# Loading two of batch 0's head pairs in two stretches and computing the first-half exponentials first, in a fused attention and feed-forward kernel

## The chip, the cores and the metric

The kernel runs on one core of one Trainium2 chip. The metric is the device time of one execution in microseconds (us). Shorter is better. All runs told here were fast runs: the kernel uses one core, and no run lay over 1.5% above the fastest of its kernel.

The engines are named as in the profile: PE is TensorE's matmul, PEld its weight load, DVE VectorE, ACT ScalarE, POOL GpSimd. "The granted clock" is TensorE's clock in the records, as a share of full speed. L318 is line 318 of the kernel that the line is read from. The change shifts lines by some 20: what is L494 (up-projection), L519 (down product), L298 (values product), L243 (scores), L446 (broadcasts), L439 (XT) and L502 (HT) in the kernel before is L518, L543, L318, L263, L470, L463 and L526 in the changed one.

## The reference, cut to what matters

```python
# q, k, v: 8 batches x 8 heads x 576 tokens x 64, float32
scores = (q @ k.T) / sqrt(64)          # a block of 64 tokens sees itself and all earlier blocks
attn   = softmax(where(block_i >= block_j, scores, -1e9))
x      = (attn @ v)                    # 4608 tokens x 512, heads side by side
xn     = x / sqrt(mean(x*x) + 1e-6) * rms_g
out    = (silu(xn @ w_gate) * (xn @ w_val)) @ w_out      # 512 -> 1536 -> 512
```

## The kernel before

All heavy products are bf16 on TensorE. Heads are worked on in four pairs of two. For batch 0 the exponentials of a pair come in three steps; "a" holds all that the first 256 working tokens need, which are called the first half here. (The working order puts block 0 last, so token 64 is the first.)

```python
"a": ([(0, 64, 256, 0), (1, 128, 192, 256), (2, 256, 64, 448)], 0, 512),
"b": ([(0, 320, 256, 0), (1, 320, 256, 256)], 512, 512),
"c": ([(2, 320, 256, 0), (3, 384, 192, 256)], 1024, 448),
```

The mask is applied afterwards: in each exponential's result the corner blocks that must not count are set to zero by VectorE. `clear()` issues all corner memsets that are pending, and `clear_pair` those of one pair, right ahead of its values product. A group is one piece of the feed-forward part, one `ffn_up` or one `ffn_down`; `later(k, ...)` puts work off by k groups.

```python
def values_mm(b, t, part=WHOLE, early=False):
    clear_pair(b, t)                    # memsets on VectorE, if any are pending
    ...                                 # the matmuls of PT and V
def ffn_up(n, m, k, lo, w):
    ...                                 # 16 matmuls on TensorE (8 of WG, 8 of WV)
    # tanh on ScalarE -> gs on VectorE -> HT on VectorE
def group(n=1):
    ...                                 # one ffn_up or one ffn_down
    clear()                             # stands behind gs and HT in VectorE's order
    ...                                 # then the work that later(k, ...) put off by k groups
```

The order of the opening, from the first half's norm on:

```python
outs = values_mm(0, 0, SECOND, early=True)
scores(0, 3, "c")
outs += values_mm(0, 1, SECOND, early=True)
fill(3)                                 # matmuls on zeros, only to keep TensorE at work
for u in range(HP): norm_scale("a", 0, 0, 256, u)      # broadcasts (TensorE), XT (VectorE)
mark(256)                               # groups of the first 256 tokens may run now
evacuate(outs, True)
clear()
group()
...                                     # head product, values of pairs 2 and 3
group()
norm_sums("b", 0, SECOND)               # the second half's norm: sums, squares, turn, ratio
...
later(1, norm_root, "b");   later(1, norm_newton, "b", 0)
later(2, norm_newton, "b", 1); later(2, norm_spread, "b")
group(); transpose_pair(1, 0, on_act="qk"); group()
scores(1, 0, 0); scores(1, 0, 1)
group()
scores(1, 0, 2)
transpose_pair(1, 1, on_act="qk")
for u in range(HP): norm_scale("b", 0, 256, 320, u)    # needs st of the second norm
mark(S)
scores(1, 1, 0)
group()
```

There are six groups on the first half's tokens. The seventh needs the second half's XT.

The softmax here doesn't subtract the row's maximum and nothing guards it: scores larger than these inputs give would overflow.

Of the kernel before, what the change touches and what calls it, by code (L numbers as in the profile page):

```python
# [13 lines left out]
ALU = mybir.AluOpType  # L14
# [3 lines left out]
def kernel(  # L18
# [44 lines left out]
    SECOND = ([(0, 512, 256, 0), (1, 768, 256, 0), (2, 1024, 256, 0), (3, 1280, 192, 64),  # L63
               (4, 0, 64, 192)], 256, 256)
    PW = 1472
    WARM = 11

    const = ctx.enter_context(tc.tile_pool(name="const", bufs=1))
    nat = ctx.enter_context(tc.tile_pool(name="nat", bufs=20))
    qkt = ctx.enter_context(tc.tile_pool(name="qkt", bufs=2))  # L70
    ppool = ctx.enter_context(tc.tile_pool(name="ppool", bufs=5))
    p4pool = ctx.enter_context(tc.tile_pool(name="p4pool", bufs=2))
# [35 lines left out]
    def load_pair(b, t):  # L108
        for kind, src in (("q", q), ("k", k)):
            NAT[kind, b, t] = nt = nat.tile([P, S], BF16, name="nt")  # L110
            nc.gpsimd.dma_start(
                out=nt, in_=src[b, 2 * t:2 * t + 2].rearrange("h (p x) d -> (h p) (x d)", x=TPP))

    def load_chunk(b, c):
        rows = P if c < 4 else BLK
        for kind, src in (("q", q), ("k", k)):
            NAT[kind, b, c] = nt = nat.tile([P, S], BF16, name="nt")
            nc.gpsimd.dma_start(  # L118
                out=nt[0:rows, 0:512].rearrange("p (h d) -> p h d", h=H),
                in_=src[b, :, c * P:c * P + rows, :].rearrange("h p d -> p h d"))  # L120
# [28 lines left out]
    fill(WARM)  # L149
    load_pair(0, 0)  # L150
    make_identity(nc, ident)
    for t in range(1, HP):
        load_pair(0, t)
    for c in range(5):
        load_v(0, c)
    nc.scalar.dma_start(out=gscale, in_=moe_rms_g.rearrange("(c p) -> p c", p=P))

# [13 lines left out]
    for t in range(HP):  # L171
        for a in range(2):
            r = 32 * t + a
            nc.vector.tensor_copy(out=SELB[:, t, a * D:(a + 1) * D],
                                  in_=ident[:, r:r + 1].to_broadcast([P, D]))


    nc.gpsimd.memset(GSUM, 0.0)
    for i in range(4):
        nc.gpsimd.affine_select(  # L180
            out=GSUM.rearrange("p (j i) -> p j i", j=4), in_=GSUM.rearrange("p (j i) -> p j i", j=4),
            pattern=[[0, 4], [-1, 32]], base=-32 * i, channel_multiplier=1,
            compare_op=ALU.not_equal, fill=1.0 / DM)


    QT, KT = {}, {}
# [2 lines left out]
        QT[b] = qkt.tile([P, HP, S], BF16, name="QT")  # L189
        KT[b] = qkt.tile([P, HP, S], BF16, name="KT")  # L190

    def transpose_pair(b, t, on_act=""):
        if t == 0:
            alloc_t(b)
        for dst, kind in ((QT[b], "q"), (KT[b], "k")):
            src = NAT.pop((kind, b, t))
            pt = ps_f.tile([P, 1024], BF16, name="fps")
            for x in range(TPP):
                for a in range(2):
                    r = slice(a * D, (a + 1) * D)  # L200
                    nc.tensor.transpose(pt[r, x * BLK:(x + 1) * BLK],  # L201
                                        src[r, x * D:(x + 1) * D], ident[r, r])
            o = dst[:, t, :].rearrange("p (s x) -> p s x", x=TPP)
            i = pt[:, 0:S].rearrange("p (x s) -> p s x", x=TPP)
            if kind in on_act:
                nc.scalar.copy(out=o, in_=i)  # L206
            else:
                nc.vector.tensor_copy(out=o, in_=i)  # L208
# [23 lines left out]
    def scores(b, t, step):  # L232
        scores_exp(*scores_mm(b, t, step))
# [28 lines left out]
    def scores_ends(b):  # L262
        scores_exp(*scores_ends_mm(b))  # L263
# [42 lines left out]
    def head_product(b, oh):  # L306

        for u in range(HP):
            for a in range(2):
# [3 lines left out]
                                 start=True, stop=True, skip_group_check=True)  # L313
        return (OT[b][:, :, 512:S], SQ[b][:, :, 512:S],
                oh[:, 0:HP * BLK].rearrange("p (t d) -> p t d", t=HP))

    def evacuate(outs, early=False):
        for o, sq, i in outs:  # L318
# [304 lines left out]
        load_pair(1, t)  # L623
    for c in range(5):
        load_v(1, c)
    fill(2)
    scores(0, 0, "a")
    scores(0, 0, "b")
    transpose_pair(0, 1, on_act="k")
    scores(0, 0, "c")  # L630
    fill(1)
    scores(0, 1, "a")
    transpose_pair(0, 2)
    scores(0, 1, "b")
    clear()
    fill(2)
    scores(0, 2, "a")
    transpose_pair(0, 3)
    clear()
    scores(0, 1, "c")  # L640
    values(0, 0, FIRST, early=True)
    scores(0, 3, "a")
    outs = values_mm(0, 1, FIRST, early=True)
    scores_ends(0)
    evacuate(outs, True)
    clear()
    values(0, 2, FIRST, early=True)
    scores(0, 2, "b")
    values(0, 3, FIRST, early=True)
    norm_sums("a", 0, FIRST)  # L650
    scores(0, 2, "c")
    fill(1)
    norm_squares("a", 0, FIRST)
    norm_turn("a")
    norm_ratio("a")
    scores(0, 3, "b")
    fill(2)
    norm_root("a")
    norm_newton("a", 0)
    norm_newton("a", 1)  # L660
    norm_spread("a")
    outs = values_mm(0, 0, SECOND, early=True)
    scores(0, 3, "c")
    outs += values_mm(0, 1, SECOND, early=True)
    fill(3)
    for u in range(HP):
        norm_scale("a", 0, 0, 256, u)
    mark(256)
    evacuate(outs, True)
    clear()  # L670
    group()
    evacuate([head_product(0, ps_f.tile([P, 512], FP32, name="fps"))], True)
    values(0, 2, SECOND, early=True)
    values(0, 3, SECOND, early=True)
    group()
    norm_sums("b", 0, SECOND)
    norm_squares("b", 0, SECOND)
# [11 lines left out]
    fetch(1, 4)  # L689
    scores(1, 0, 0)  # L690
    scores(1, 0, 1)
    group()
    scores(1, 0, 2)
    transpose_pair(1, 1, on_act="qk")
    for u in range(HP):
        norm_scale("b", 0, 256, 320, u)
    mark(S)
    scores(1, 1, 0)
    group()
    transpose_pair(1, 2, on_act="qk")  # L700
# [22 lines left out]
    clear()  # L723
    group()
    values(1, 3, early=True)
    later(1, tail, 1, 4)
    for _ in range(5):
        group()
        fetch(3, 2)
# [103 lines left out]
```

## Time and profile before

| | before |
|---|---|
| time, median of 4 runs | 389.25 us (388.91 to 390.56) |
| span of the profiled run | 387.5 us |
| busy: PE, DVE, ACT | 97%, 67%, 49% |
| first group starts | 25.44 us |
| transposes of batch 1's pair 2 start | 44.33 us |
| first tanh of the second block of 512 tokens | 79.66 us |

The last three rows are points in the run at which the two kernels can be laid beside each other. The following row of the page gives the granted clock in 40 equal slices of the span, in tenths, 9 being full speed:

```profile
PEclk9999999999999999999999999999999999999999
```

In this run TensorE is at full clock in every slice (mean 1.000), and with 97% busy it is the bound. What it waited for between 20 and 60 us, the costliest three (engine and line, what it waited for: us in total, times, longest):

```profile
PE fps L446 <- DVE XT L439: 0.8, 2, 0.5
PE fps L446 <- DVE HT L502: 0.5, 1, 0.5
PE fps L394 <- DVE w L381: 0.5, 1, 0.5
```

No single wait is longer than 0.5 us.

### The profile page before, as it was taken

What the parts mean: (1) busy time and instruction counts of PE and PEld (TensorE: products, weight loads), DVE (VectorE), ACT (ScalarE), POOL (GpSimd) and SP (SyncE); (2) the same over time, 40 slices, a digit from 0 to 9 for tenths busy, and PEclk for the clock granted to TensorE, in tenths of its full rate; (3) what the DMA queues carried; (4) which work ended last, traced back from release to release, by engine and by line L of the source; (5) the groups of instructions that cost most, each with busy time, mean ns of one, the idle gap of its engine ahead of it and who ended that gap; (6) DMA issues with size and microseconds to landing.
All of it is one profiled execution on the core that took longest, in us unless ns stands there. A gap on an engine that the chain in (4) does not pass through costs nothing.

```text
span 387.5 us, 7757 instructions
## 1 busy us (share of the span) xinstructions
PE 375.6 (97%) x3050; PEld 182.7 (47%) x3050; DVE 259.7 (67%) x620; ACT 189.3 (49%) x270; POOL 128.6 (33%) x181
## 2 busy tenths in 40 slices
PE   8789999999999999999999999999999999999996
PEld 3458666443444444444444444444444444444443
DVE  4688668377887787378967685489776848554530
ACT  3824882277556645465556454546542233332322
POOL 8926865755418302494030733400100110100000
PEclk9999999999999999999999999999999999999999
DMA  8999999999979919999960999702100220100113
GB/s 104 168 201 195 189 149 152 155 179 153 136 110 109 129 20 147 162 114 135 149 98 6 84 176 178 117 0 79 52 4 30 87 90 9 27 28 29 54 37 100
DMA packets 143364, 40.11 MB, mean 104 GB/s; under 512 B 129504, under 2 KB 140640, under 8 KB 143328
## 3 DMA queue, kind: packets, MB, share of 16 engines
q0 software_dynamic: 108448, 26.75, 72.3%
q1 hardware_dynamic: 34192, 12.74, 20.5%
q8 instruction: 24, 0.39, 0.4%
q10 hardware_dynamic: 688, 0.13, 0.2%
q14 instruction: 12, 0.10, 0.1%
HBM read 41.75 MB, written 10.17 MB: 134 GB/s over the span
## 4 chain that ended last, share of the span: by engine, by line
PE 86%; DVE 8%; ACT 4%; issue 1%; DVEq 0%
PE fps L494 45%; PE fps L519 24%; PE sps L243 5%; PE fps L298 5%; PE fps L338 3%; DVE HT L502 2%; ACT PT L256 2%; DVE gs L500 2%; PE fps L147 1%; ACT th L498 1%; PE fps L201 1%; DVE XT L439 1%; PE fps L446 1%; PE fps L360 0%; ACT KT L206 0%
## 5 line engine op out<-in xcount | busy, mean ns | idle before, releaser
L500 DVE SCALAR_TENSOR_TENSOR gs<-th,fps 128x512 bf16<-128x512 f32 x108 | 74.1, 686 | 60.6 <-ACT th L498 59.5
L494 PE MATMUL fps<-XT,WG 128*128 128x512 bf16 (+1 forms) x480 | 111.7, 359 | 0.6 <-DVE HT L502 0.5
L494 PE MATMUL fps<-XT,WV 128*128 128x512 bf16 (+1 forms) x480 | 111.0, 358 | 0.1
L256 ACT ACTIVATE PT<-sps 128x1024 bf16<-128x1024 f32 (+1 forms) x96 | 93.2, 990 | 22.5 <-PE sps L243 22.3
L519 PE MATMUL fps<-WO,HT 128*128 128x512 bf16 (+1 forms) x444 | 97.0, 373 | 0.0
L498 ACT ACTIVATE th<-fps 128x512 f32<-128x512 f32 x108 | 64.7, 599 | 63.1 <-PE fps L494 62.0
L502 DVE TENSOR_TENSOR HT<-gs,fps 128x512 bf16<-128x512 bf16 x108 | 74.3, 688 | 12.0 <-DVE gs L500 0.9
L494 PEld LDWEIGHTS <-WV 128*128 128x128 bf16 x480 | 47.0, 98 | 46.9 <-issue 0.8
L494 PEld LDWEIGHTS <-WG 128*128 128x128 bf16 x480 | 43.3, 98 | 48.3 <-issue 9.7
L519 PEld LDWEIGHTS <-HT 128*128 128x128 bf16 x444 | 42.7, 98 | 49.5 <-issue 1.7
L521 ACT ACTIVATE osb<-fps 128x512 f32<-128x512 f32 (+1 forms) x37 | 21.7, 586 | 75.3 <-PE fps L519 73.1
L523 POOL DMA_DIRECT2D out_dram<-osb x22 | 12.6, 573 | 132.7 <-ACT osb L521 129.0
L125 POOL DMA_DIRECT2D VB<-in_v_dram x48 | 39.7, 846 | 3.8 <-PE sps L243 1.1
L243 PE MATMUL sps<-QT,KT 64*128 64x192 bf16 (+5 forms) x280 | 30.8, 307 | 2.5 <-DVE KT L208 1.0
L118 POOL DMA_DIRECT2D nt<-in_q_dram x30 | 26.3, 876 | 7.0 <-DMA VB<-in_v_dram 5.3
L118 POOL DMA_DIRECT2D nt<-in_k_dram x30 | 26.3, 876 | 4.7 <-PE fps L494 2.4
L298 PE MATMUL fps<-PT,VB 128*64 128x192 bf16 (+5 forms) x280 | 25.3, 308 | 0.5 <-DVE PT L225 0.4
L527 POOL DMA_DIRECT2D out_dram<-osb x12 | 6.5, 548 | 55.7 <-ACT osb L521 55.7
L298 PEld LDWEIGHTS <-VB 128*64 128x64 bf16 x344 | 14.9, 110 | 12.1 <-issue 7.0
L243 PEld LDWEIGHTS <-KT 64*128 64x128 bf16 x280 | 9.3, 94 | 22.0 <-issue 15.7
L320 DVE CAST OT<-fps 128x512 bf16<-128x512 f32 (+1 forms) x34 | 19.0, 562 | 0.4
L475 DVE SCALAR_TENSOR_TENSOR XT<-OT,gscale,bc 128x576 bf16<-128x576 bf16 (+2 forms) x24 | 15.7, 713 | 2.2 <-DMA bc<-rows 2.1
(71 smaller groups left out, 201.3 us busy)
## 6 DMA issues: line engine op xcount, KB each, us to landing
out_dram<-osb POOLq DMA_DIRECT2D x22, 256.0 KB, 2.4
VB<-in_v_dram POOLq DMA_DIRECT2D x32, 128.0 KB, 6.1
nt<-in_q_dram POOLq DMA_DIRECT2D x24, 128.0 KB, 6.9
nt<-in_k_dram POOLq DMA_DIRECT2D x24, 128.0 KB, 7.5
bc<-rows SPq DMA_DIRECT2D x10, 288.0 KB, 4.9
WG<-in_moe_w_gate_dram POOLq DMA_DIRECT2D x4, 384.0 KB, 9.3
WV<-in_moe_w_val_dram POOLq DMA_DIRECT2D x4, 384.0 KB, 10.5
WO<-in_moe_w_out_dram POOLq DMA_DIRECT2D x4, 384.0 KB, 7.7
```

The source lines that it names most:

```text
L118: nc.gpsimd.dma_start(out=nt[0:rows, 0:512].rearrange("p (h d) -> p h d", h=H), in_=src[b, :, c * P:c * P + rows, :].rearrange("h p d -> p ...
L125: nc.gpsimd.dma_start(out=vb[r:r + n, cc, :].rearrange("p (h d) -> p h d", h=H), in_=v[b, :, tok:tok + n, :].rearrange("h p d -> p h d"))
L243: nc.tensor.matmul(sp[:, a, o:o + w], KT[b][r, t, c * P:(c + 1) * P], QT[b][r, t, q0:q0 + w], start=True, stop=True, skip_group_check=True)
L256: nc.scalar.activation(out=pt[:, :, lo:lo + width], in_=sp[:, :, 0:width], func=AF.Exp, scale=SCALE)
L298: nc.tensor.matmul(ov[a * D:(a + 1) * D, o:o + w], vb[:, c, h * D:(h + 1) * D], rhs, start=(i == 0), stop=(i == len(chunks) - 1), skip_gro ...
L320: nc.vector.tensor_copy(out=o, in_=i)
L494: nc.tensor.matmul(acc[:, i * w:(i + 1) * w], wt[c][:, p, r * P:(r + 1) * P], XT[:, p, x0:x0 + w], start=(p == 0), stop=(p == HP - 1), ski ...
L498: nc.scalar.activation(out=th, in_=g, func=AF.Tanh, scale=0.5)
L500: nc.vector.scalar_tensor_tensor(out=gs, in0=th, scalar=1.0, in1=g, op0=ALU.add, op1=ALU.mult)
L502: nc.vector.tensor_mul(out=HT[n][:, m:m + k, lo:lo + w], in0=gs.rearrange("p (k w) -> p k w", k=k), in1=u.rearrange("p (k w) -> p k w", k=k))
L519: nc.tensor.matmul(po[:, 0:step], HT[n][:, m, i * P:(i + 1) * P], WO[:, m, o:o + step], start=(m == 0), stop=(m == NMC - 1))
L521: nc.scalar.mul(out=osb[:, o:o + step], in_=po[:, 0:step], mul=0.5)
```

## The change

Its intent is to start the first group sooner. It needs the norm of 256 tokens, and for these only the first 320 loaded tokens of pairs 2 and 3 count. So those two pairs are loaded as a first and a second stretch, V's first chunks go ahead of the second stretch, and "a" of all four pairs is computed ahead of "b" and "c". What is pushed back runs between the groups. In addition, four groups instead of two now stand ahead of the second norm, its scaling stands ahead of the seventh group, and batch 1's tail is no longer put off by a group.

```diff
+    CUT = 5 * BLK
-    for t in range(1, HP):
-        load_pair(0, t)
-    for c in range(5):
+    load_pair(0, 1)
+    load_stretch(0, CUT)
+    for c in range(3):
+        load_v(0, c)
+    load_stretch(CUT, S)
+    for c in range(3, 5):
         load_v(0, c)
  ...                      (GSUM is built on VectorE, not on GpSimd)
+    transpose_pair(0, 2, "", 0, CUT)
+    scores(0, 1, "a")
+    transpose_pair(0, 3, "", 0, CUT)
+    scores(0, 2, "a")
+    fill(1)
+    scores(0, 3, "a")
  ...                      (four values products of the first half, squares, norm a,
                            second transposes of pairs 2 and 3, end blocks)
     for u in range(HP):
         norm_scale("a", 0, 0, 256, u)
     mark(256)
-    evacuate(outs, True)
+    copy(outs)            # ScalarE in place of VectorE
     clear()
-    group()
-    evacuate([head_product(0, ps_f.tile([P, 512], FP32, name="fps"))], True)
-    values(0, 2, SECOND, early=True)
-    values(0, 3, SECOND, early=True)
+    scores(0, 2, "b")
+    group()
+    outs = values_mm(0, 1, SECOND, early=True)
+    scores(0, 2, "c")
+    copy(outs)
+    scores(0, 3, "b")
+    group()
+    outs = [head_product(0, ps_f.tile([P, 512], FP32, name="fps"))]
+    outs += values_mm(0, 2, SECOND, early=True)
+    scores(0, 3, "c")
+    copy(outs)
+    group()
+    copy(values_mm(0, 3, SECOND, early=True))
     group()
     norm_sums("b", 0, SECOND)
  ...
     scores(1, 0, 1)
-    group()
-    scores(1, 0, 2)
-    transpose_pair(1, 1, on_act="qk")
     for u in range(HP):
         norm_scale("b", 0, 256, 320, u)
     mark(S)
+    group()
+    scores(1, 0, 2)
+    transpose_pair(1, 1, on_act="qk")
     scores(1, 1, 0)
  ...
-    later(1, tail, 1, 4)
+    tail(1, 4)
```

More of the change, by code (lines that the diff above doesn't have):

```diff
@@ L65 @@
     PW = 1472
+    CUT = 5 * BLK
     WARM = 11
     const = ctx.enter_context(tc.tile_pool(name="const", bufs=1))
-    nat = ctx.enter_context(tc.tile_pool(name="nat", bufs=20))
+    nat = ctx.enter_context(tc.tile_pool(name="nat", bufs=16))
+    nat2 = ctx.enter_context(tc.tile_pool(name="nat2", bufs=2))
     qkt = ctx.enter_context(tc.tile_pool(name="qkt", bufs=2))
@@ L112, in load_pair, with load_stretch @@
                 out=nt, in_=src[b, 2 * t:2 * t + 2].rearrange("h (p x) d -> (h p) (x d)", x=TPP))
+    def load_stretch(lo, hi):
+        for kind, src in (("q", q), ("k", k)):
+            if lo == 0:
+                nt = nat2.tile([P, 2, S], BF16, name="nt2")
+                NAT[kind, 0, 2], NAT[kind, 0, 3] = nt[:, 0, :], nt[:, 1, :]
+                NAT[kind] = nt
+            for a in range(2):
+                nc.gpsimd.dma_start(
+                    out=NAT[kind][a * D:(a + 1) * D, :, lo:hi],
+                    in_=src[0].rearrange("(t h) s d -> h t s d", h=2)[a, 2:HP, lo:hi, :].rearrange(
+                        "t (p x) d -> p t (x d)", p=BLK))
     def load_chunk(b, c):
@@ L175, with make_gsum @@
                                   in_=ident[:, r:r + 1].to_broadcast([P, D]))
-    nc.gpsimd.memset(GSUM, 0.0)
-    for i in range(4):
-        nc.gpsimd.affine_select(
-            out=GSUM.rearrange("p (j i) -> p j i", j=4), in_=GSUM.rearrange("p (j i) -> p j i", j=4),
-            pattern=[[0, 4], [-1, 32]], base=-32 * i, channel_multiplier=1,
-            compare_op=ALU.not_equal, fill=1.0 / DM)
+    def make_gsum():
+        one = small.tile([P, 32], FP32, name="one")
+        nc.vector.tensor_reduce(out=one, in_=ident.rearrange("p (j i) -> p i j", j=4),
+                                op=ALU.add, axis=mybir.AxisListType.X)
+        nc.vector.tensor_single_scalar(
+            GSUM.rearrange("p (j i) -> p j i", j=4),
+            one.unsqueeze(1).to_broadcast([P, 4, 32]), 1.0 / DM, op=ALU.mult)
     QT, KT = {}, {}
@@ L190, in alloc_t, with transpose_pair @@
         KT[b] = qkt.tile([P, HP, S], BF16, name="KT")
-    def transpose_pair(b, t, on_act=""):
+    def transpose_pair(b, t, on_act="", lo=0, hi=S):
+        x = (hi - lo) // BLK
         if t == 0:
@@ L195, in transpose_pair @@
         for dst, kind in ((QT[b], "q"), (KT[b], "k")):
-            src = NAT.pop((kind, b, t))
+            src = NAT[kind, b, t][:, lo:hi]
             pt = ps_f.tile([P, 1024], BF16, name="fps")
-            for x in range(TPP):
+            for i in range(x):
                 for a in range(2):
                     r = slice(a * D, (a + 1) * D)
-                    nc.tensor.transpose(pt[r, x * BLK:(x + 1) * BLK],
-                                        src[r, x * D:(x + 1) * D], ident[r, r])
-            o = dst[:, t, :].rearrange("p (s x) -> p s x", x=TPP)
-            i = pt[:, 0:S].rearrange("p (x s) -> p s x", x=TPP)
+                    nc.tensor.transpose(pt[r, i * BLK:(i + 1) * BLK],
+                                        src[r, i * D:(i + 1) * D], ident[r, r])
+            o = dst[:, t, lo:hi].rearrange("p (s x) -> p s x", x=x)
+            i = pt[:, 0:hi - lo].rearrange("p (x s) -> p s x", x=x)
             if kind in on_act:
@@ L315, in head_product, with copy @@
                 oh[:, 0:HP * BLK].rearrange("p (t d) -> p t d", t=HP))
+    def copy(outs):
+        evacuate(outs)
     def evacuate(outs, early=False):
@@ L625 @@
         load_v(1, c)
+    nc.vector.memset(KT[0][:, 2:HP, CUT:3 * P], 0.0)
     fill(2)
@@ L628 @@
     scores(0, 0, "b")
-    transpose_pair(0, 1, on_act="k")
-    scores(0, 0, "c")
-    fill(1)
-    scores(0, 1, "a")
-    transpose_pair(0, 2)
-    scores(0, 1, "b")
-    clear()
-    fill(2)
-    scores(0, 2, "a")
-    transpose_pair(0, 3)
-    clear()
-    scores(0, 1, "c")
-    values(0, 0, FIRST, early=True)
-    scores(0, 3, "a")
-    outs = values_mm(0, 1, FIRST, early=True)
-    scores_ends(0)
-    evacuate(outs, True)
-    clear()
-    values(0, 2, FIRST, early=True)
-    scores(0, 2, "b")
-    values(0, 3, FIRST, early=True)
-    norm_sums("a", 0, FIRST)
-    scores(0, 2, "c")
-    fill(1)
+    fill(1)
+    transpose_pair(0, 1)
+    make_gsum()
+    transpose_pair(0, 2, "", 0, CUT)
+    scores(0, 1, "a")
+    transpose_pair(0, 3, "", 0, CUT)
+    scores(0, 2, "a")
+    fill(1)
+    scores(0, 3, "a")
+    clear_pair(0, 0)
+    clear_pair(0, 1)
+    outs = values_mm(0, 0, FIRST, early=True)
+    outs += values_mm(0, 1, FIRST, early=True)
+    for o, sq, i in outs:
+        nc.vector.tensor_copy(out=o, in_=i)
+    outs = values_mm(0, 2, FIRST, early=True)
+    outs += values_mm(0, 3, FIRST, early=True)
+    nc.vector.tensor_mul(out=SQ[0][:, 0:2, 0:256], in0=OT[0][:, 0:2, 0:256],
+                         in1=OT[0][:, 0:2, 0:256])
+    for o, sq, i in outs:
+        nc.scalar.activation(out=sq, in_=i, func=AF.Square)
+        nc.vector.tensor_copy(out=o, in_=i)
+    norm_sums("a", 0, FIRST)
+    scores(0, 0, "c")
     norm_squares("a", 0, FIRST)
@@ L655 @@
     norm_ratio("a")
-    scores(0, 3, "b")
-    fill(2)
+    clear()
+    transpose_pair(0, 2, "qk", CUT, S)
+    fill(1)
     norm_root("a")
@@ L661 @@
     norm_spread("a")
+    transpose_pair(0, 3, "qk", CUT, S)
+    fill(1)
+    scores_ends(0)
+    scores(0, 1, "b")
     outs = values_mm(0, 0, SECOND, early=True)
-    scores(0, 3, "c")
-    outs += values_mm(0, 1, SECOND, early=True)
-    fill(3)
+    scores(0, 1, "c")
+    fill(2)
     for u in range(HP):
@@ L668 @@
     mark(256)
-    evacuate(outs, True)
+    copy(outs)
     clear()
+    scores(0, 2, "b")
     group()
-    evacuate([head_product(0, ps_f.tile([P, 512], FP32, name="fps"))], True)
-    values(0, 2, SECOND, early=True)
-    values(0, 3, SECOND, early=True)
+    outs = values_mm(0, 1, SECOND, early=True)
[9 more added lines that the diff above has]
+    copy(values_mm(0, 3, SECOND, early=True))
     group()
@@ L691 @@
     scores(1, 0, 1)
+    for u in range(HP):
+        norm_scale("b", 0, 256, 320, u)
+    mark(S)
     group()
@@ L694 @@
     transpose_pair(1, 1, on_act="qk")
-    for u in range(HP):
-        norm_scale("b", 0, 256, 320, u)
-    mark(S)
     scores(1, 1, 0)
```

## The prediction

> **What bounds the kernel now.** I read four views. First the page: TensorE is busy for 97% of 387.5 us at full clock, so a change of order can win only time in which TensorE stands still or runs matmuls on zeros.
>
> ```profile
> PE 375.6 (97%) x3050; PEld 182.7 (47%) x3050; DVE 259.7 (67%) x620; ACT 189.3 (49%) x270; POOL 128.6 (33%) x181
> ```
>
> Then the busy time of each engine in stretches that I chose at the turning points of the opening (start:end, length, then each engine):
>
> ```profile
> 7.70:16.82 9.12, 7.10 (x185) 4.57 (x186) 5.34 (x16) 8.10 (x10) 8.55 (x15) 1.00 1.74 155
> 16.82:25.44 8.62, 6.95 (x84) 3.73 (x84) 6.48 (x27) 4.31 (x5) 4.39 (x8) 1.00 1.31 202
> 25.44:44.33 18.89, 17.52 (x266) 13.62 (x266) 15.71 (x44) 9.56 (x14) 12.72 (x19) 1.00 1.52 192
> 44.33:76.06 31.73, 31.22 (x364) 19.31 (x364) 19.65 (x51) 15.36 (x22) 19.62 (x25) 1.00 1.96 158
> 78.42:370.00 291.58, 290.64 (x2019) 131.28 (x2018) 204.80 (x456) 144.26 (x209) 74.80 (x100) 1.00 0.79 89
> ```
>
> Length less PE is idle time: 2.0, 1.7, 1.4 and 0.5 us. After 78.42 there is 0.9 us in 291, so delay there passes to the end nearly one for one. The same view of the tile of zeros shows 3.5 us of filler between 6.0 and 25.4. With 0.2 us before 7.7 and 0.4 between 76.06 and 78.42, idle time is 6.2 us up to 78.42; with filler 9.6. That is the ceiling of any gain: 2.5%.
>
> Third, the chain of waits from 5 to 50 us shows what sets the first group of up-projections, which starts at 25.44:
>
> ```profile
> 15.74 1.03 ACT PT L256
> ...
> 19.31 0.46 DVE tr L369
> ...
> 23.26 0.46 DVE st L424
> ...
> 24.07 1.33 DVE XT L439 x3
> 25.40 0.04 issue
> 25.44 1.11 PE fps L494 x8
> ```
>
> The norm of the first 256 tokens needs all four pairs' first exponentials. The one of pair 3 starts at 15.74, the norm's transpose (tr) at 19.31, XT at 24.07. Until then TensorE has little else.
>
> Fourth, the timeline. Pair 3's data land at about 11.5 (issue at 5.69 plus 5.8), but its transposes run at 13.31; so loading is not what holds pair 3, order is. V's third chunk, issued at 8.32, lands 6.1 us later at 14.4, which does hold the first values product (14.30).
>
> **What the Trainium skill says.** "Perfetto Trace Analysis", Identifying the Most-Contended Engine: TensorE's busy share is no measure of nearness to its peak. I use the busy figure only to find gaps. "DMA: Bandwidth & Descriptors", Specifications: full rate needs pieces of at least 512 B. The new stretches write 640 and 512 B a piece in place of 1152 B; no transfer of this shape is in the trace, so I take the old rate. "ScalarE: Activation LUTs", Step-by-step: 0.833 ns an element whatever the function. The trace agrees: exponentials of 1024 and 896 columns take 1031 and 924 ns, 0.84 ns a column. "TensorE: Matmul & The Clock Gate", Part 1: after a window of about 3.4 us idle TensorE halves its clock. Here 11 fillers take 4.87 us (0.44 each), two later ones 0.60 together. No gap that I expect below reaches 3.4 us.
>
> **The change, part by part.** Times are estimates from durations of this trace.
>
> *Loads.* Transfers of 144 KB land 0.70 us apart (8.0 to 11.5 for five). The first stretches (320 KB after pair 1, complete at 8.8) come down in 1.55 us, at 10.3 to 10.5. 256 KB then move behind V, so V's third chunk lands 1.2 us sooner, at 13.2. Weights keep their place: four more issues of 0.55 us are paid by the GSUM work (1.7 us) that leaves GpSimd.
>
> *Norm a.* Pair 1's K copy goes from ScalarE to VectorE (9.7 to 10.4), GSUM takes some 0.7 us there, then four copies of 320 columns at 0.45: done at 12.95. Pair 3's first exponential can run from 13.5 to 14.5 instead of 15.74 to 16.77. The corners, four values products, the squares (two now on ScalarE, some 0.4 us each, ready at 16.1) and four matmuls put tr at 16.8: 2.5 us earlier. From tr to st 4.4 us pass as before (19.31 to 23.72): st at 21.2. But TensorE's order now has behind it the second transposes, the end blocks, a score, pair 0's second values product, and another score that waits for the end blocks' exponential (ScalarE: 00c, four copies of 256 columns at 0.37, ends: to 20.7). It reaches the broadcasts at 22.1, not 21.2. XT starts at 22.4, and the first group at about 23.8, 1.6 us earlier than 25.44.
>
> *Work put off.* What TensorE now has after that start and before had ahead of it: one values product (0.56) and three scores (0.3 each), 1.5 us. So up to here the change wins 0.1 us: the start is earlier, but less has been done.
>
> *From the first group to pair 2 of batch 1.* Two more up groups (1.85 us each, spacing of the unhindered groups) stand in this stretch; with them before would reach these transposes at 44.33 + 3.70 = 48.03. New waits:
> (a) ScalarE between the first groups gets three exponentials and OT copies that VectorE did before (0.4 each). The tanh of the second group waits behind two exponentials and a copy, and the third group's accumulator comes free about 0.55 us late.
> (b) The scaling of the second norm now stands right after the sixth group, which is the last with tokens to work on; before, groups of the first half covered it. In before a group started at 35.01 and the second norm's st was ready at 39.44, 4.43 us later, because VectorE does HT first and then Newton. The same order follows the sixth group here. TensorE has its 1.85 us and 0.52 of scores, then waits 2.05; then four XT of 0.48 us each go on before the seventh group, which reads just those tokens. Beside 0.7 us of broadcasts TensorE idles 3.3 us.
> (c) Pair 1's scores of batch 1 directly follow its transposes. They wait for an exponential (0.92) and two copies (0.64 each) on ScalarE: 1.6 us. Before, the scaling stood between and the two waits overlapped.
> Together 5.5 us where before idled 1.4: 4.1 lost.
>
> *Batch 1's norm.* It starts one group sooner in calls, but since two groups more have run, three down products follow its sums and not four. From its root to st took 3.5 us (70.52 to 74.0), one down product covers 2.67 plus 0.36 of root: 0.45 us of wait. Of scores beside XT one fewer is there: 0.3. Sum 0.75.
>
> Balance: -0.1 + 4.1 + 0.75 = +4.7 us, 394.0. I put it at 393.5, as some of these waits may overlap.
>
> **The rivals.** *The early start is kept.* If group, scaling and scores closed up, the 1.6 us earlier start and three fewer fillers (8 for 11) would show as 1 to 2 us: 387.5. For it: idle time of 3.7 us ahead of the first group; against it: the deferred 1.5 us and the order of the second norm, which the trace of before already times. *Transfers become the bound.* Half-height loads with shorter pieces could land 1 us late, or WG and WV: WV's first part lands at 13.9 + 7.5 = 21.4 and the last at 18.3 + 14.3 = 32.6, while the groups that need them are due at 23.8 and some 36. So weights have 2 us of room; a late first stretch would move norm a and add up to 1 us: 395. *ScalarE becomes the bound of the opening.* It does the same exponentials, 13 in all, and gains copies; if the exponentials lie further behind than in (a), each group up to the fourth waits about 0.5 us: 395.5. *The clock drops* in the 3.3 us of (b): up to 3.4 us at half rate adds 1.7. The granted clock of before speaks against it.
>
> **Range and chances.** Without (a), and with 1 us more won ahead of the first group: about 391. With late loads and more ScalarE waiting: 396 to 397. Range 390.3 to 396.5. A gain of 2% (7.8 us) would need most of the ceiling of 9.6, and the 7.3 us of it ahead of the first group hardly shrink by the steps above. A loss of 2% needs all of the above and a rival. Chances 0.01, 0.92, 0.07.
>
> **What would show it.** tr of the first norm near 16.8 and the first group near 23.8; a wait of TensorE's broadcasts for st of about 2 us after the sixth group, and the seventh group 4 us after the sixth ends; the scores after pair 1's transposes of batch 1 waiting 1.6 us for the KT copy; the third group 0.5 us late behind ScalarE. The prediction is wrong if the seventh group follows with under 2 us of idle time, if the first group starts before 22.8, or if TensorE gains idle or lost time after 85 us.

## The result, and the profile after

| | before | after |
|---|---|---|
| time, median of 4 runs | 389.25 us | 400.43 us (400.14 to 401.41) |
| span of the profiled run | 387.5 | 398.4 |
| first group starts | 25.44 | 24.29 |
| transposes of batch 1's pair 2 | 44.33 (48.03 with two more groups of 1.85) | 56.53 |
| first tanh of the second block | 79.66 | 88.86 |

The ratio is 1.0285, with a 95% interval of 1.0255 to 1.0315: the changed kernel is slower by 2.9%. All outputs are right. A ratio here and below is the mean time of one kernel's fast runs over that of the other's of the same rounds, so it is not quite the ratio of the medians that are quoted.

The page of the changed kernel first: busy time of the engines, and the granted clock in 40 slices.

```profile
PE 376.4 (94%) x3009; PEld 183.8 (46%) x3047; DVE 258.1 (65%) x616; ACT 192.4 (48%) x280; POOL 130.2 (33%) x180
...
PEclk9989999999999999999999999999999999999999
```

TensorE has about the same busy time as before, but its share of the span is down from 97% to 94%: the loss is mostly waiting. Two things in the small print matter. The third slice of the clock shows 8 and not 9; and 41 matmul records fewer are in the trace (3009 against 3050). Three of them are fillers that the change takes out, the others are missing, but not before 57 us, where every up group is there in full; so only a busy sum of the late part is too low.

Next, the stretches that answer those of the prediction: up to the first group, from there to the transposes of pair 2, on to the scaling of batch 1, and the rest. The columns are start:end, length, busy time of PE, PEld, DVE, ACT and POOL, then granted clock, DMA share and GB/s.

```profile
7.91:24.29 16.38, 12.77 (x243) 7.63 (x245) 11.11 (x41) 10.36 (x16) 13.00 (x19) 0.90 1.44 153
24.29:56.53 32.24, 24.63 (x322) 18.06 (x321) 17.21 (x44) 15.62 (x24) 19.73 (x27) 0.95 1.60 187
56.53:85.24 28.71, 27.67 (x329) 16.14 (x331) 17.06 (x47) 14.50 (x21) 10.27 (x14) 1.00 1.47 106
90.06:380.90 290.84, 286.85 (x1974) 130.57 (x2006) 203.59 (x454) 143.71 (x208) 75.98 (x101) 1.00 0.82 88
```

The second row is the place. It holds 7.6 us in which TensorE is not busy (32.24 less 24.63), where the stretch of before held 1.4. And the clock is below 1.0 in the first two rows. The same view of TensorE's waits from 20 to 60 us as above:

```profile
PE fps L318 <- DVE PT L245: 3.2, 2, 1.7
PE fps L470 <- DVE st L448: 2.1, 1, 2.1
PE sps L263 <- ACT KT L226: 1.5, 1, 1.5
```

The second and third are the waits of the prediction's steps (b) and (c). The first is not in the prediction at all: the values products of pairs 2 and 3 wait for VectorE's writes to PT, and those are the corner memsets. The chain of waits of the changed kernel shows what stands in front of them (start us, us, what):

```profile
27.18 0.92 ACT PT L276
28.09 0.26 ACT OT L346
28.36 0.93 ACT PT L276
29.29 0.50 ACT th L522
29.81 0.70 DVE gs L524
...
30.60 0.69 DVE HT L526
...
31.34 0.12 DVE PT L245
31.50 0.30 PE fps L318 x3
...
44.85 0.69 DVE HT L526
...
46.28 0.52 DVE st L448
46.84 0.31 PE fps L470
47.17 1.93 DVE XT L463 x4
49.15 2.69 PE fps L518 x13
...
53.76 0.55 ACT KT L226
54.36 0.39 PE sps L263 x2
```

At 31.34 a memset of 0.12 us ends TensorE's wait. The exponential "c" of pair 2 that it corrects is issued between the first and the second group, so its corner is still pending when the second group is issued, and is cleared by that group's closing `clear()`: behind gs and HT in VectorE's order. The gs waits for the tanh, and the tanh stands on ScalarE behind two exponentials and a copy (27.18 to 29.29). The same happens to pair 3's corner at 35.67, where the tanh stands behind one exponential and two copies. Before, these corners were cleared ahead of the first group. Further down the chain the scaling goes directly from st to the four XT to the seventh group, and then the K copy holds the scores of pair 1.

The clock, in stretches of 3.5 us around its two drops (columns as above):

```profile
17.20:20.70 3.50, 2.71 (x60) 1.75 (x54) 2.54 (x12) 2.18 (x6) 3.34 (x5) 1.00 1.25 187
20.70:24.20 3.50, 3.02 (x23) 1.32 (x18) 2.27 (x9) 2.24 (x4) 1.09 (x2) 0.51 1.31 200
44.50:48.00 3.50, 1.20 (x9) 0.58 (x6) 2.87 (x9) 1.83 (x2) 3.09 (x4) 1.00 1.24 201
48.00:51.50 3.50, 3.14 (x15) 1.83 (x14) 1.56 (x4) 0.60 (x1) 1.40 (x3) 0.51 1.35 192
```

The second row of each couple ran at half clock. In the last, 3.14 us of busy time did what would take about 1.6 at full clock. So the "x13" of the seventh group took 2.69 us where a whole group of 16 matmuls takes 1.85.

Finally, the run gets slower once more where the prediction saw nothing. The offset between the two kernels is 9.2 us at the first tanh of the second block, and stays there until about 155 us, where it grows by 0.9, and at about 235 us by 0.8. The waits of the changed kernel's TensorE after 100 us show this; before had no such line:

```profile
PE fps L543 <- DVE HT L526: 1.0, 2, 0.5
```

A down product is the next group behind the up group whose HT it reads, with only scores, values and head products between. The two waits are 1.0 us of the 1.7. In the same places the head product also starts some 0.3 us later than before, which no run explains. The 9.2 and 1.7 us make up the 10.9 us by which the spans differ.

### The profile page after: what moved, and what is told of

Read it like the earlier page. It is cut to its first block, busy times and chain, and to the rows that moved or that the text cites. A ratio compares the mean times of both kernels' runs of the same rounds, so it can differ in the third digit from the quotient of the medians.

```text
span 398.4 us, 7715 instructions
## 1 busy us (share of the span) xinstructions
PE 376.4 (94%) x3009; PEld 183.8 (46%) x3047; DVE 258.1 (65%) x616; ACT 192.4 (48%) x280; POOL 130.2 (33%) x180
## 4 chain that ended last, share of the span: by engine, by line
PE 81%; DVE 9%; ACT 4%; issue 2%; POOL 2%; DMA 1%; DVEq 0%; POOLq 0%
PE fps L518 42%; PE fps L543 23%; PE sps L263 5%; PE fps L318 5%; PE fps L362 3%; DVE HT L526 2%; DVE gs L524 2%; ACT PT L276 2%; DVE XT L463 2%; DMA VB<-in_v_dram 1%; ACT th L522 1%; DVE st L448 1%; POOL nt L124 1%; PE fps L470 1%; PE fps L384 1%
## 5 line engine op out<-in xcount | busy, mean ns | idle before, releaser
L543 PE MATMUL fps<-WO,HT 128*128 128x512 bf16 (+1 forms) x433 | 95.7, 373 | 1.4 <-DVE HT L526 1.0
L318 PEld LDWEIGHTS <-VB 128*64 128x64 bf16 x344 | 15.1, 110 | 17.2 <-issue 11.0
L346 ACT CAST OT<-fps 128x512 bf16<-128x512 f32 (+1 forms) x15 | 7.6, 515 | 23.3 <-PE fps L318 23.3
## 6 DMA issues: line engine op xcount, KB each, us to landing
WV<-in_moe_w_val_dram POOLq DMA_DIRECT2D x4, 384.0 KB, 10.9
```

The costliest lines, as they stand in the source:

```text
L318: nc.tensor.matmul(ov[a * D:(a + 1) * D, o:o + w], vb[:, c, h * D:(h + 1) * D], rhs, start=(i == 0), stop=(i == len(chunks) - 1), skip_gro ...
L543: nc.tensor.matmul(po[:, 0:step], HT[n][:, m, i * P:(i + 1) * P], WO[:, m, o:o + step], start=(m == 0), stop=(m == NMC - 1))
```

## The experiments

Rival causes after this reading: the corner memsets (3.15 us of wait: 1.72 and 1.43), the halved clock, the st wait of the second norm (2.07), the K copy's wait (1.51), the batch 1 tail, the opening's order, and the late waits for HT. The medians of the kernel before were 389.28 to 389.44 us in these experiments. "Opening" is the part up to the first group.

**1. Corners cleared early (on the changed kernel).**

```diff
     scores(0, 2, "c")
+    clear()
     copy(outs)
...
     scores(0, 3, "c")
+    clear()
     copy(outs)
```

> The corner memsets of pair 2's and pair 3's last step are put on VectorE before the next group's HT, not behind it. Theory (TensorE waits 1.72 + 1.43 us for these memsets because VectorE works in order, and nothing else holds it there): both waits vanish and the time falls by about 3.1 us, to 397.3; the third up group starts near 30.6 and the fourth near 33.0 in place of 32.0 and 36.1. Rival (ScalarE is the bound of these groups, as the prediction had it, and the memset only came last): under 1 us is won, 399.5 or more, and the wait goes to ScalarE's copies.

Measured: 398.50 us (397.43 to 399.17), ratio 1.0233 [1.0210, 1.0256]. TensorE's waits from 20 to 60 us in this run now begin with:

```profile
PE fps L470 <- DVE st L448: 2.1, 1, 2.1
PE sps L263 <- ACT KT L226: 1.5, 1, 1.5
PE fps L518 <- DVE XT L463: 0.4, 2, 0.2
PE fps L518 <- DVE gs L524: 0.4, 1, 0.4
```

The wait for PT is gone, the other two are unchanged. The last line is new: the third group waits 0.36 us (at 32.64) for gs, which sets its accumulator free. That is the wait of the prediction's step (a), which the corners had hidden. From the first group's start to the fourth's took 8.69 us (26.35 to 35.04) against 11.78 (24.29 to 36.07): 3.1 us, as the theory has it. The time fell by only 1.9, since the clock was worse: in the profiled run it was half for some four times as long as at each of the drops above.

```profile
12.90:26.60 13.70, 12.51 (x141) 6.88 (x141) 7.38 (x30) 6.92 (x14) 8.93 (x14) 0.50 1.36 171
```

The first group started 2.06 us later for it. That the clock moves this start shows from five runs (experiments 1, 2, 3, 6 and 7) whose code is the change's own up to the first group: it starts at 26.35, 26.11, 23.91, 25.01 and 23.36 us in their profiles, for 24.29 in the change, and the half clock lies at 12.9 to 26.6, 14.6 to 24.8, 15.3 to 18.7, 12.8 to 23.1 and 11.6 to 18.5, for 20.7 to 24.2. So the clock isn't the same from one run to the next, and a time of a few runs blurs a cause of 1 or 2 us. The points in the trace must be read with it.

**2. Second norm's st earlier.**

```diff
-    later(2, norm_newton, "b", 1)
-    later(2, norm_spread, "b")
+    later(1, norm_newton, "b", 1)
+    later(1, norm_spread, "b")
```

> Newton's second step and the spread of norm b go ahead of the sixth group's gs and HT on VectorE. Theory (the stall at the second scaling is VectorE's whole queue: gs and HT of the sixth group and then four XT): st is ready near 44.9 and not 46.8, but XT still has to follow HT near 46.4, so only about 0.8 us is won, 399.6. Rival (st alone is the wait): the whole wait of 2.07 us goes, 398.3. If the clock of TensorE no longer halves after it, 1.1 us more in either case.

Measured: 399.68 us (398.40 to 401.92), ratio 1.0268 [1.0221, 1.0315]. The timeline of TensorE in this run (start, us, what, and in brackets the idle time before it and its releaser) shows the four broadcasts of the scaling:

```profile
47.31 0.87 PE L470 MATMUL fps<-st,SELB 128*128 128x320 bf16 x3 [0.48 <-DVE st L448]
48.68 0.30 PE L470 MATMUL fps<-st,SELB 128*128 128x320 bf16 x1 [0.50 <-DVE HT L526]
```

The st wait shrank from 2.07 to 0.48, but VectorE now does HT behind st and XT behind HT. From the sixth group to the seventh took 4.72 us (44.41 to 49.13) instead of 5.41 (42.36 to 47.77): 0.7 us, not 1.6. VectorE has the same work in another order, so most of the wait only moves.

**3. The seventh group behind scores and transposes.**

```diff
     mark(S)
-    group()
     scores(1, 0, 2)
     transpose_pair(1, 1, on_act="qk")
+    group()
     scores(1, 1, 0)
```

> The seventh group is moved from ahead of batch 1's scores and pair 1's transposes to behind them, so that it hides both the XT pacing and the KT copy. Theory (the wait of 1.51 us for the KT copy and about 1 us of XT pacing are idle time made by the order alone): 2.5 us is won, 397.9, and with an undisturbed clock in that group 1.1 more, 396.8. Rival (the group's tanh then stands behind the copies and exponentials on ScalarE and the loss moves to the eighth group): under 1 us.

Measured: 397.91 us (396.06 to 399.60), ratio 1.0219 [1.0176, 1.0263]; the verdict at 2% is unclear. The st wait stays at 2.07, the K copy's wait before pair 1's scores is gone, and the sixth group's start to the transposes of pair 2 took 10.5 us in place of 14.2. In this run the clock did not drop in that stretch, so the 3.7 us are the two together; it dropped at 15.3 and at 32.3 instead. The four runs' mean clocks were 0.979 to 0.995, and their times differ by 3.5 us.

**4. Fillers at the two places of the drop.**

```diff
     transpose_pair(0, 2, "qk", CUT, S)
-    fill(1)
+    fill(4)
...
     transpose_pair(0, 3, "qk", CUT, S)
-    fill(1)
+    fill(2)
...
     scores(1, 0, 1)
+    fill(9)
```

> Fillers are added only where TensorE waits: 3 and 1 more after the second transposes of pairs 2 and 3, 9 before the second scaling. Theory (the granted clock fell to half at 20.7 to 24.2 and 48.0 to 51.5 because TensorE did too little in the 3.5 us before): the clock stays at 1.0, the seventh group ends about 1.1 us earlier and the first about 0.6: 398.7. Rival (the clock falls whatever the filler, or falls a window later): same time as the change within 0.5 us, and the mean clock stays below 1. The waits for the corner memsets, st and KT stay as they are.

Measured: 399.03 us (398.42 to 399.54), ratio 1.0249 [1.0230, 1.0268]. The two drops went, but others came at 11.5 to 18.4 and 32.0 to 35.4 us. The gain is 1.4 us, and the theory is half right: fillers hold the clock where they stand, but the places with too little work are more than two.

**5. Fillers at every hole.** As in 4, and also: 2 each behind pair 2's first transposes, behind pair 3's, ahead of and behind `scores(0, 3, "a")`, ahead of the first values product of pair 2; 6 ahead of the head product, 5 ahead of the second values product of pair 3, and 6 ahead of `scores(1, 1, 0)`.

> The change with fillers at every place where TensorE waits up to the scores of batch 1's second pair: 7 more between 9 and 15 us, 4 more near 18, and before the corner waits, the second scaling and the KT copy. No data wait is removed. Theory (the halved clock, 7 to 17 us of it in a run, is a cost of its own, and it comes from the thin work of TensorE in the opening): the clock stays at 1.0 in every run, the spread of the runs shrinks, and the time falls to about 397; the waits for PT corners, st and KT stay. Rival (the clock is no cost because TensorE waits for others in those stretches anyway): 400 within 0.7 us, or the clock still falls.

Measured: 397.98 us (397.69 to 398.42), ratio 1.0220 [1.0200, 1.0239]. The mean granted clock is 1.0 in all runs. The two stretches up to and after the first group:

```profile
7.60:23.40 15.80, 14.54 (x252) 7.80 (x248) 10.79 (x40) 10.20 (x16) 13.13 (x19) 1.00 1.42 146
23.40:54.78 31.38, 29.26 (x348) 19.82 (x346) 17.37 (x45) 15.62 (x24) 18.89 (x26) 1.00 1.54 189
```

The halved clock thus cost 2.4 us in the median, and the fillers themselves run in time in which TensorE would wait. In the traces, the first group starts at 23.40 for 24.29 us, and from the sixth group to the transposes of pair 2 takes 13.08 (41.70 to 54.78) for 14.17: the two drops of the change cost 0.9 and 1.1. The spread of the times shrank too, which makes this the better ground to measure on.

**6. Batch 1's tail put off again.**

```diff
-    tail(1, 4)
+    later(1, tail, 1, 4)
```

> Batch 1's norm is put back behind the next group, as before the change. Theory (only four down products are there to hide it, and the change has spent one of them already, so the earlier call is a repair within the change): one down product fewer hides the norm, TensorE waits up to 2.7 us longer for st ahead of batch 2, 402.5. Rival (the earlier call is itself a loss of the change): 399.5 or less.

Measured: 402.51 us (402.32 to 404.30), ratio 1.0349 [1.0322, 1.0376]. TensorE waits 3.0 us for st in the stretch from 60 to 100 us, where the changed kernel waits 0.4. The immediate tail repairs some 2 us of what the shift by two groups would cost (part of the 2.1 can be the clock: the four runs' means were 0.974 to 0.982); it is no cause of the loss.

**7. The order of before for the second norm.** Corners as in 1; three groups in place of four ahead of the second norm; then the order of the kernel before.

```diff
     copy(values_mm(0, 3, SECOND, early=True))
-    group()
     norm_sums("b", 0, SECOND)
...
     scores(1, 0, 1)
-    for u in range(HP):
-        norm_scale("b", 0, 256, 320, u)
-    mark(S)
     group()
     scores(1, 0, 2)
     transpose_pair(1, 1, on_act="qk")
+    for u in range(HP):
+        norm_scale("b", 0, 256, 320, u)
+    mark(S)
     scores(1, 1, 0)
```

> Corner memsets early as in e1, three groups and not four ahead of norm b, and from there the order of before: second scaling behind the scores and pair 1's transposes, with the sixth group ahead of them. The loads and the opening of the change stay. Theory (the losses behind the opening are the order's, not the loads'): waits for PT (3.15), st (2.07) and KT (1.51), some 1 us of XT pacing and 0.7 of the norm of batch 1 go, 8.4 us together, 392, and 1 us less if the clock does not fall. Rival (the opening itself costs the time, through the clock or through the work put off): 396 or more.

Measured: 392.19 us (391.80 to 393.86), ratio 1.0088 [1.0059, 1.0117], as expected. Corners and order, together with what clock they bring with them, are 8.2 us of the 11.2.

**8. The same with the fillers of 5 in the opening.**

> e7 with the opening's fillers of e5. Theory: the clock stays at 1.0 and the rest is as in e7, 390.5; first group near 24, sixth before 42. If e7 and e8 have the same time, the clock is no cost of the change; if e8 is over 392, the opening loses time in another way than by clock.

Measured: 391.81 us (391.50 to 392.04), ratio 1.0063 [1.0047, 1.0079], clock 1.0. Only 0.4 us came of it, where 390.5 us was expected. The clock did drop in the runs of 7 (means of 0.981 to 0.996), but not where it costs much. In the profiled run of 7 it was half in this stretch alone:

```profile
11.60:18.50 6.90, 6.11 (x80) 3.31 (x79) 4.11 (x18) 4.22 (x7) 6.90 (x11) 0.51 1.48 135
```

Its first group starts at 23.36 us, that of 8, at full clock, at 23.60, and both take 23.2 us more to the transposes of pair 2. So this drop cost nothing that shows, and a mean clock alone doesn't tell what is lost. The two late waits of the down products for HT are still there, with the same line as above.

**9. One group fewer behind batch 1's tail (on 8).**

```diff
     tail(1, 4)
-    for _ in range(5):
-        group()
+    for i in range(5):
+        if i < 4:
+            group()
         fetch(3, 2)
```

> e8 with one group call fewer ahead of batch 2, the call that found nothing to do, so that from batch 2 on ups and downs interleave with the attention as before the change. Theory (the loss after 90 us, 1.7 us in the change, in e7 and in e8 alike, comes from the shift of groups against the attention, where two down products wait 0.5 us each for HT): both waits for HT go and 1.5 us is won, 390.3. Rival (the late loss is of another kind, as buffers of the loads): 391.8 as e8.

Measured: 390.21 us (389.92 to 391.62), ratio 1.0028 [1.0006, 1.0050]. The waits for HT are gone after 100 us, and the offset to before is 0.9 us from 80 us to the end. So the late loss came of the number of `group()` calls between batch 1's tail and batch 2's scores; it is 1.6 us in the median.

**10. Scores of the opening moved up (on 9).** `scores(0, 0, "c")` goes ahead of "a" of pair 1, and "b" and "c" of pairs 1 to 3 each take the place of the one before, so that two fillers' places and two waits hold scores.

```diff
     transpose_pair(0, 2, "", 0, CUT)
-    fill(2)
+    scores(0, 0, "c")
     scores(0, 1, "a")
...
-    fill(2)
+    scores(0, 1, "b")
     outs = values_mm(0, 2, FIRST, early=True)
...
-    scores(0, 0, "c")
+    scores(0, 1, "c")
     norm_squares("a", 0, FIRST)
```

> e9 with three scores moved into waits of the opening in place of fillers: pair 0's last and pair 1's middle one among the first exponentials, where ScalarE idles 0.9 and 1.3 us, the later ones one place up. Theory (the opening of the change wins nothing because its earlier first group has less work done behind it): the work put off falls by 1 us at the same first group near 23.5, 389.3, level with the kernel before. Rival (the exponentials push the first halves' chain back): first group near 25, 390.5 or more.

Measured: 389.85 us (389.35 to 391.98), ratio 1.0015 [0.9993, 1.0038]. The timeline of TensorE shows a new wait: batch 1's first transposes wait for their load.

```profile
35.46 0.47 PE L221 MATMUL fps<-ident,nt 64*64 64x64 bf16 x18 [0.67 <-DMA nt<-in_q_dram]
```

The exponentials now come in time, and the next limit appears.

**11. V behind both stretches (on 8).**

```diff
     load_stretch(0, CUT)
-    for c in range(3):
-        load_v(0, c)
     load_stretch(CUT, S)
-    for c in range(3, 5):
+    for c in range(5):
         load_v(0, c)
```

> e8 with all of V behind both stretches. Theory (V ahead of the rest is worth what its third chunk lands earlier, since the first values products wait for it): about 1.2 us later tr, first group near 24.8, of which some 0.8 us reaches the end: 392.6. Rival (V's place is hidden behind the exponential of pair 3): 391.8 as e8.

Measured: 392.78 us (392.56 to 392.97), ratio 1.0083 [1.0063, 1.0103]. The norm's transpose (tr) comes at 18.07 instead of 17.54 us, the first group at 24.12 instead of 23.60, and the time is 1.0 us longer than that of 8. V's place ahead of the second stretch is worth about 1 us.

**12. The kernel before without its 11 fillers after the warm-up.** All six `fill` calls of the opening are taken out.

> The kernel before without its 11 fillers of the opening (the warm-up of 11 stays). Theory (fillers keep the clock at 1.0, and thin work in the opening halves it): the clock falls to half for 3.5 to 14 us in most runs, and the time is 1 to 3 us longer, 391, with a wider spread. Rival (the clock falls only in the change's order): clock 1.0 and the time of before or up to 0.5 us less.

Measured: 391.75 us (391.15 to 392.79), ratio 1.0060 [1.0036, 1.0084]. The clock:

```profile
12.60:16.00 3.40, 3.30 (x60) 2.12 (x60) 2.38 (x11) 2.32 (x3) 3.40 (x6) 0.50 2.13 142
22.90:29.70 6.80, 5.24 (x30) 3.04 (x32) 4.81 (x16) 0.85 (x2) 2.12 (x4) 0.50 1.31 203
```

The old kernel drops as well once its fillers are gone, and loses 2.3 us against 389.44. Its clock of 1.0, on which the prediction relied, was the work of its fillers, and not quite safe with them: six of its runs have mean clocks of 0.991 to 0.995 and took 389.9 to 391.5 us. The change has eight in the opening where before had eleven.

**13. Batch 1's first pair loaded ahead of the last weights (on 10).**

```diff
-    for j in range(4):
+    for j in range(3):
         load_up(j)
-    for t in range(HP):
+    load_pair(1, 0)
+    load_up(3)
+    for t in range(1, HP):
         load_pair(1, t)
```

> e10 with batch 1's first pair issued ahead of the last third of WG and WV. Theory (the earlier first group has met the next bound, the landing of that pair at about 35.4 and 36.1, while the last weights land near 34 and are used at 39): the wait of 1.1 us goes and the time falls by about 1 us, to 388.8, 0.6 us under the kernel before. Rival (the fifth group then waits for its weights, or the XT and HT waits behind it take up what is won): 389.8 as e10.

Measured: 389.29 us (388.66 to 390.91), ratio 0.9998 [0.9971, 1.0025]; the load wait is gone. It is level with the kernel before (389.28 us), not below it as expected. The first group starts at 23.45, 2.0 us sooner than before, but at the first tanh of the second block the two stand at 79.70 and 79.66 us. By then all of the earlier start is spent: between the two points TensorE is busy for 1.7 us more than before (53.62 for 51.94) and idle for 0.35 more. The values product and the score that still run behind the start would be some 0.9 of the 1.7, by the prediction's durations; the rest isn't split.

**14. Corners on the clocked ground of 5.** As 5, with the two `clear()` of 1, without the fillers that stood in the two waits for the corners.

> e5 with the corner memsets early as in e1 and without the 11 fillers that stood in those two waits. Clock 1.0. Theory: 3.1 us less than e5, 394.9. Rival (ScalarE's copies and exponentials then hold these groups): 396.5 or more.

Measured: 396.05 us (394.97 to 396.80), ratio 1.0163 [1.0136, 1.0191]. From the first to the fourth group took 8.90 us (24.92 to 33.82) against 12.01 in 5: again 3.1 us. The median moved by 1.9 only, since without all fillers the clock fell again, at 11.1 to 14.5 us in the profiled run.

**15. As 14, with the seventh group moved as in 3** and without the six fillers ahead of `scores(1, 1, 0)`.

> e14 with the seventh group behind batch 1's scores and pair 1's transposes as in e3. Clock 1.0. Theory: the wait for KT (1.51) and the XT pacing of the seventh group (1.0) go, 2.5 us less than e14, 392.4; st's wait of 2.07 stays, filled. Rival: 394 or more.

Measured: 392.53 us (392.43 to 394.05), ratio 1.0084 [1.0057, 1.0111]: 3.5 us less than 14, where 2.5 were expected. From the sixth group's start to the transposes of pair 2 it took 10.50 us (38.35 to 48.85) where 14 takes 13.09 (40.10 to 53.19): 2.6 us, as expected. The rest is the drop in 14's opening, whose first group starts at 24.92 us and not at 23.16. Moving one call past a scores call and a pair of transposes was, after the corners, the largest repair.

**The ledger**, by medians from 400.43 us down: fillers (5) 2.4 us, corners (14) 1.9 net of a drop of the clock, the seventh group's place (15) 3.5, the whole of before's order for the second norm (8) 0.7, the late waits (9) 1.6, early scores and pair load (10, 13) 0.9. That leads to 389.29. Neighbours in this list differ in small ways besides, so each term is good to perhaps 1 us. At points in the traces the corners are 3.1 and the seventh group's place 2.6: the drop in 14 took from the one and gave to the other.

## Why the prediction was wrong

The prediction said 393.5 us with a range up to 396.5 and gave "within 2%" a chance of 0.92. Measured were 400.43 us, slower by 2.9%. Its direction and several of its steps were right; what failed is the following.

**Step (a), "ScalarE between the first groups", failed.** It saw that the tanh would stand behind two exponentials and a copy, and put 0.55 us on it, for an accumulator that comes free late. The lateness was there, but its victim was another: the corner memsets behind gs and HT on VectorE, and behind them the values products of pairs 2 and 3. That is 3.15 us, a term that the prediction's sum lacks, and experiments 1 and 14 both take 3.1 us away with two early `clear()` calls. Once they are gone, the accumulator's wait is there too, with 0.36 us. I had followed each matmul to the engine that does its exponential, but not to the memset that also writes its operand.

**The rival "the clock drops" was dismissed, and came true.** "The granted clock of before speaks against it" was no argument: experiment 12 shows that before's clock depended on its fillers, of which the change takes some away while it makes more holes. And the prediction looked only for a gap of 3.4 us; the drops came with no single wait over 2.07 us. It put the cost at 1.7 us at most; experiment 5 makes it 2.4.

**No late loss was foreseen.** The prediction says that TensorE gaining idle time after 85 us would prove it wrong, and it did: 1.7 us around two down products, of which 1.0 is their wait for HT; experiment 9 removes all of it by taking out one group.

The sum nearly closes. For the transposes of pair 2 the prediction comes to 48.03 − 0.1 + 4.1 = 52.0 us; they were at 56.53, 4.5 us later. Of these 2.6 are the corners (3.15 less 0.55), 1.1 the half clock at the seventh group (by experiment 5), and 0.5 the first group (24.29 for 23.8), which is itself late by the clock (23.40 in experiment 5); 0.3 has no name. The half clock takes less than half of its 3.14 busy us, since the first matmuls there would have waited for XT anyway (in experiment 5 they do, 0.2 us at a time). With 1.7 us late, 4.7 + 4.5 + 1.7 give the 10.9 us of the spans.

What held:

- *The opening.* tr came at 17.11 (16.8 predicted), the first group at 24.29 (23.8). The first stretches landed 4.0 to 4.3 us after their issue, at about 9.9 (10.3 to 10.5 predicted), so the shorter pieces cost nothing that shows. V's third chunk was late: its matmuls start at 14.15, after a wait of 0.21 us for it, where 13.2 was predicted. Apart from that "transfers become the bound" was rightly set aside. (The prediction's 0.84 ns a column is what each further column of an exponential adds; the 1024 columns of 1031 ns are 1.0 ns each.)
- *Work put off.* That the earlier start would be all but cancelled by the values product and the scores pushed behind it fits experiment 13, where the earlier start of 2.0 us is worth nothing at 80 us. It doesn't test the -0.1 us by itself, since two of the three scores had moved ahead of the start again.
- *Steps (b) and (c).* The waits for st (2.07, predicted 2.05) and for the K copy (1.51, predicted 1.6) are in the trace as drawn. But experiment 2 shows that the st wait isn't worth its own length: of the 1.6 us taken from it, VectorE's order gives back 0.9. And one move takes away 2.6 us at full clock (15), or 3.7 with the drop of the clock (3), though it leaves st's wait as it is.
- *Batch 1's tail.* The st wait of 0.42 us is there (0.45 predicted). The offset grew by 0.7 us from the transposes of pair 2 to the first tanh of the second block, for 0.75 predicted.

What stays open: by which rule the clock is halved isn't shown. Before had 2.35 us of busy time in the 3.4 us from 10.0 to 13.4 and kept its clock, and the changed kernel had 2.71 in the 3.5 from 17.2 (0.61 of it transposes and 0.78 fillers) and lost it. Since experiments 1 to 4 each met another clock, their times alone can't split the loss; the split rests on the points in the traces and on the runs with fillers.

## What to carry to other kernels

When exponentials, masks or copies are moved between groups of matmuls, follow every writer of each operand, small ones too: here a memset of 0.12 us that stood behind gs and HT cost TensorE 1.72 us. An earlier start of the first matmul is worth only what it does not push behind it; compare the two kernels at a point behind all the moved work. And when a change takes out fillers or makes holes, don't take the old kernel's full clock for granted: put fillers in the holes, and then measure the rest.

## What the Trainium skill lacked or had wrong

- "TensorE: Matmul & The Clock Gate", Part 1 and "Why this matters for your kernels": the advice is to leave no idle gap over about 3 us between bursts. Here the clock halved with no wait above 2.07 us, after stretches of 3.5 us in which TensorE was busy for 1.20 and even for 2.71 us. The same page's section "A second HAM failure mode" says that frequent small idle times also make the gate oscillate, which fits better, and which I should have used; it gives no number for how much work is enough, and none is shown here either.
- The same page says that the cold start differs from run to run, but has no figure for how much the times of one kernel scatter when the clock drops in its midst: experiment 3 had mean clocks of 0.979 to 0.995 and times of 396.06 to 399.60 us, and with fillers at every hole (experiment 5) 397.69 to 398.42 us.
- No page that I used names small VectorE writes to a matmul's operand as a wait to look for when an order is changed: here TensorE waited 1.72 us for a memset of 0.12 us, which stood behind gs and HT.
